# Attention and FFN in one kernel: FFN buffers lent to exponential tiles, one activation table, down weights loaded late, planner constants set again

## The chip, the cores and the metric

The kernel runs on one core of one Trainium2 chip. The metric is the device time of one execution in microseconds (us). "Span" is the time between the first and the last instruction of the profiled execution; it is about 2.1 us shorter than the time of the same run.

Names: PE is the TensorE matmul row, DVE is VectorE, ACT is ScalarE, POOL is GpSimd, SP is the engine that issues most DMAs. PEclk is the granted TensorE clock as a share of full speed.

## The reference, cut to what matters

```python
# x: [1, 2048, 512], bf16.  32 heads of 16.  F = 1376
g = sigmoid((x * gate_w).sum(-1, keepdims=True))
q, k, v = split_heads(x @ wqkv)
a = softmax(q @ k.T * Dh ** -0.5) @ v @ wo          # 32 heads, 2048 x 2048 scores each
b = ((x @ w_gate) * (x @ w_up)) @ w_down
return g * a + (1 - g) * b
```

The exponentials rule: 32 x 2048 x 2048 of them. The kernel works on score tiles of 128 keys by 512 queries; a "quarter" `m` is four heads and 512 queries, and there are 32 quarters of 64 tiles, 2048 tiles in all.

## The kernel before

The kernel is a Python program that plans itself. While it is built, a small list scheduler walks a clock for each engine, decides what each engine does next, and emits the instructions in that order. That fixes the order of each engine, and between engines the program waits on semaphores (in the trace of before ScalarE waits four times, 10.1 us in all, for PV matmuls in the first 200 us).

Of the tiles of each quarter a fourth is meant for VectorE and the rest for ScalarE:

- ScalarE takes two or three score tiles per instruction from PSUM, computes Exp and writes bf16 tiles into "cells" of `PT`. In the plan it has `NA = 3 * 16 * 32 = 1536` tiles.
- VectorE makes the other 512 by integer arithmetic on the bf16 bits: one base tile and three shifted copies, on VectorE and GpSimd. Two such tiles share pairs of cells.
- If VectorE falls behind, a tile of its share is handed over to ScalarE (`convert`).
- The PV matmuls read the cells and free them. ScalarE cannot start while no run of free cells is there (`alloc`).

```python
NMAIN = 54                      # cells in PT, 512 columns each
NCELL = NMAIN + 4               # and the four tiles of wv, once V is done
RA = 26                         # cells 0..25 ScalarE's, 26..53 VectorE's pairs
...
segs = [(0, RA), (NMAIN, 4)]
def alloc(n, t, pair=False, keep=0):
    if pair: ...                # first free pair of cells from RA on
    ...                         # ScalarE: smallest free run of n cells in segs
...
def act_step():                 # ScalarE's step of the planner
    ...
    c = alloc(n, t)
    if c is None:
        return False            # no free cells: ScalarE waits
    old = claim(c, n, 1)        # waits for the PV matmuls that read these cells last
    k = _Task("act", [sc] + old, lambda a: a.activation(cell_ap(c, n), src, ACT.Exp, scale=LN2 / 128.0), ...)
...
lag = lag_()                    # how far VectorE's share is behind ScalarE's
if dleft and lag > LC:
    convert()                   # hand one of VectorE's tiles to ScalarE
```

Projections, the gate, FFN and output projection are "fills": they are put between the score matmuls at positions counted in ScalarE tiles (`ua`), from `F0` (first FFN fill) to `F1`. `FA0` and `FA1` say how late a fill may be before it takes the third score bank of a slot. The gate is one fill of 64 matmuls with one output column each:

```python
for t in range(16):
    for kt in range(4):
        e.matmul(bk.ap[:, t : t + 1], xT[:, kt, t * 128 : (t + 1) * 128], gw[:, kt : kt + 1], ...)
```

The last quarter does without the round trip through memory that spreads the reciprocals in the others (in e1 one took 11.05 us from its first transfer to the multiply). It takes them from a PSUM sum with Ln and Exp, in four blocks:

```python
for tt in range(4):             # four output-projection fills on PE first
    o_first.append(pe_run(deps, fn, ...))
for tt in range(4):
    a1 = now("act", [lastpv, free], lambda a: a.activation(lnd[:, cs], DB.ap[:, cs], ACT.Ln), 0.2)
    a2 = now("act", [a1], lambda a: a.activation(rlast[:, cs], lnd[:, cs], ACT.Exp, scale=-1.0), 0.2)
    mt = now("dve", [a2], lambda v: v.tensor_tensor(OX[..., cs], psO[:, cs], rlast[:, cs], ALU.mult), 0.2)
    o = pe_run([mt], col(banks[tt].ap, OX[..., cs], woz[:, 1, :], False, True), ...)
    combine(4 * c + tt, banks[tt].ap, o)      # DVE: g * a + (1 - g) * b, then the output DMA
```

The softmax here doesn't subtract the row's maximum and nothing guards it: scores larger than these inputs give would overflow.

## Time and profile before

770.96 us, median of 4 runs (769.18 to 773.75). The profiled run took 769.67 us; it is not one of the four.

| what | value | view |
|---|---|---|
| span | 767.6 us | page |
| ACT / PE / DVE busy | 727.6 / 707.3 / 658.8 us | page |
| ACT busy, 0 to 200 us | 172.5 of 200 us | stretches |
| ACT busy, 200 to 700 us | 496.1 of 500 us | stretches |
| tiles on ScalarE | 512 x 2 + 177 x 3 = 1555 | groups by form |
| from the first Ln to the end | 767.6 - 752.15 = 15.45 us | timeline |

From 200 to 700 us ScalarE is busy 99% of the time. This stretch can only get shorter if ScalarE gets fewer tiles. The rest is at the two ends.

The waits of ScalarE in the first 200 us, from the waits view of before (engine, line, whom it waited for: total us, times, longest):

```profile
ACT PT L1446 <- PE psO L1035: 10.1, 4, 4.5
ACT PT L1446 <- PE psS L861: 9.6, 7, 5.9
...
ACT wv L1446 <- PE psS L861: 1.1, 2, 0.6
```

`PE psO L1035` is the PV matmul: ScalarE had scores and waited for a free cell, four times, 10.1 us. `PE psS L861` is the score matmul. 5.9 us of that are the start, which leaves 4.8 us.

ScalarE's exponentials, from the groups by form of before (count, busy us, mean ns, idle before):

```profile
L1446 ACT ACTIVATE PT<-psS 128x1024 bf16<-128x1024 f32 x418 | 422.6, 1128 | 14.6 <-PE psS L861 11.4 <-PE psO L1035 2.9
L1446 ACT ACTIVATE PT<-psS 128x1536 bf16<-128x1536 f32 x154 | 237.8, 1544 | 11.3 <-PE psO L1035 9.2 <-PE psS L861 1.6
L1446 ACT ACTIVATE wv<-psS 128x1024 bf16<-128x1024 f32 x94 | 102.3, 1114 | 2.1 <-PE psS L861 2.0
L1446 ACT ACTIVATE wv<-psS 128x1536 bf16<-128x1536 f32 x23 | 35.9, 1559 | 0.0
L1576 ACT ACT_TABLE_LOAD x4 | 5.1, 1283 | 0.1
L1577 ACT ACT_TABLE_LOAD x4 | 5.1, 1283 | 0.1
```

The tail of before, from its timeline (start, duration, what):

```profile
752.15 0.28 ACT L1576 ACTIVATE oraw<-psS 128x128 f32<-128x128 f32 x1 [1.20 <-PE psS L1046]
...
752.44 1.28 ACT L1577 ACT_TABLE_LOAD   x1
...
753.74 0.31 ACT L1577 ACTIVATE rb<-oraw 128x128 f32<-128x128 f32 x1
...
754.07 1.28 ACT L1576 ACT_TABLE_LOAD   x1
...
755.36 0.28 ACT L1576 ACTIVATE oraw<-psS 128x128 f32<-128x128 f32 x1
...
755.82 0.75 DVE L765 SCALAR_TENSOR_TENSOR ost<-psX,gval,wq 128x512 bf16<-128x512 f32 x1 [1.45 <-PE psX L492]
...
764.72 0.75 DVE L765 SCALAR_TENSOR_TENSOR ost<-psS,gval,wq 128x512 bf16<-128x512 f32 x1 [0.72 <-PE psS L492]
```

Every Ln and every Exp has a table load before it. From the end of Exp (754.05 us) to the start of the next Ln (755.36) are 1.31 us with the load of 1.28 inside. From one Ln to the next are 3.21 us. The first combine (755.82) waits for PE, not for ScalarE.

### The profile page before, as it was taken

The page shows a single profiled execution, that of the slowest core. Times are in us where ns is not written, and L with a number is a line of the kernel's source. Part 1 is how long each engine was busy: PE and PEld are TensorE (multiplying, and loading weights), DVE is VectorE, ACT ScalarE, POOL GpSimd, SP SyncE. Part 2 cuts the span into 40 slices and gives each one's busy share as a digit, 9 for nine tenths or more (in the row PEclk, how much of TensorE's full clock was granted, in tenths as well). Part 3 has the DMA queues.
Part 4 walks back from the last instruction along what each step waited for, and adds up shares of the span by engine and source line. Part 5 has one row for each costly group of instructions (what it writes and reads, how often), then busy time and mean ns, then how long its engine had stood idle before and what let it go on. Part 6 is the DMA issues. An engine that isn't in the chain of part 4 may idle for free. (4 is left out here: it accounts for less than half of the span.)

```text
span 767.6 us, 21608 instructions
## 1 busy us (share of the span) xinstructions
PE 707.3 (92%) x9149; PEld 207.6 (27%) x9149; DVE 658.8 (86%) x1255; ACT 727.6 (95%) x710; POOL 314.4 (41%) x334
## 2 busy tenths in 40 slices
PE   7998988988999999999999999999999998899894
PEld 3323322322222222222222222222222222222221
DVE  3889896689898999999989989898788989989882
ACT  3999988898999999999999999999999999999987
POOL 2534553144434434443434434434433334444430
PEclk9999997999999999999999999999999999999887
DMA  9800000000000010000000100000000100000000
GB/s 185 264 17 2 20 17 19 2 16 20 16 16 13 9 34 30 20 17 17 18 10 13 37 26 17 16 15 20 6 16 21 44 17 19 3 19 15 20 16 28
DMA packets 31015, 21.66 MB, mean 28 GB/s; under 512 B 18344, under 2 KB 25928, under 8 KB 30920
## 3 DMA queue, kind: packets, MB, share of 16 engines
q1 hardware_dynamic: 26936, 18.44, 8.2%
q10 hardware_dynamic: 3984, 1.84, 1.1%
q8 instruction: 73, 1.20, 0.6%
q14 instruction: 22, 0.18, 0.1%
HBM read 15.11 MB, written 2.35 MB: 23 GB/s over the span
## 5 line engine op out<-in xcount | busy, mean ns | idle before, releaser
L1446 ACT ACTIVATE PT<-psS 128x1024 bf16<-128x1024 f32 (+1 forms) x572 | 614.2, 1240 | 25.9 <-PE psS L861 13.0
L978 POOL TENSOR_SCALAR PT<-PT 128x1024 int16<-128x1024 int16 x243 | 256.1, 1055 | 359.7 <-DVE PT L975 226.4
L861 PE MATMUL psS<-QM,KE 32*128 32x512 bf16 x1732 | 272.7, 390 | 15.6 <-ACT PT L1446 7.8
L919 DVE TENSOR_SCALAR PT<-psX 128x512 int16<-128x512 f32 x316 | 216.0, 683 | 46.4 <-PE psS L861 41.6
L1035 PE MATMUL psO<-PT,VS 128*18 128x512 bf16 x1791 | 239.0, 387 | 2.6 <-POOL PT L978 1.0
L1035 PE MATMUL psO<-PT,VD 128*18 128x512 bf16 x1479 | 227.1, 387 | 4.8 <-POOL PT L978 3.4
L975 DVE TENSOR_SCALAR PT<-PT 128x1024 int16<-128x1024 int16 (+1 forms) x498 | 217.2, 476 | 6.6 <-PE psO L1035 1.2
L1446 ACT ACTIVATE wv<-psS 128x1024 bf16<-128x1024 f32 (+1 forms) x117 | 138.2, 1201 | 2.1 <-PE psS L861 2.0
L861 PE MATMUL psX<-QM,KE 32*128 32x512 bf16 x316 | 122.0, 386 | 16.7 <-ACT PT L1446 5.5
L919 DVE TENSOR_SCALAR PT<-psS 128x512 int16<-128x512 f32 x177 | 119.3, 682 | 11.8 <-PE psS L861 8.9
L861 PEld LDWEIGHTS psS<-QM,KE 32*128 32x128 bf16 x1732 | 68.0, 91 | 165.8 <-ACT PT L1446 72.0
L1035 PE MATMUL psO<-wv,VS 128*18 128x512 bf16 x257 | 71.6, 391 | 0.4 <-DVE PT L919 0.2
L1035 PEld LDWEIGHTS psO<-PT,VS 128*18 128x18 bf16 x1791 | 56.4, 89 | 57.5 <-issue 33.9
L861 PEld LDWEIGHTS psX<-QM,KE 32*128 32x128 bf16 x316 | 28.7, 91 | 144.9 <-issue 50.9
L1035 PEld LDWEIGHTS psO<-PT,VD 128*18 128x18 bf16 x1479 | 52.4, 88 | 52.5 <-issue 29.4
L492 PE MATMUL psS<-xT,wu 128*32 128x512 bf16 x672 | 54.5, 389 | 0.5 <-DVE PT L919 0.2
L492 PE MATMUL psS<-wd,hT 128*32 128x512 bf16 (+1 forms) x704 | 52.6, 384 | 1.1 <-DVE PT L919 1.1
L492 PE MATMUL psS<-xT,wg 128*32 128x512 bf16 x672 | 52.8, 385 | 0.8 <-DVE KE L521 0.3
L1107 POOL TENSOR_TENSOR OT<-oraw,rb 128x512 bf16<-128x512 f32 x16 | 20.7, 1293 | 28.7 <-DMA rb<-rscr 23.6
L707 DVE TENSOR_TENSOR hT<-psS,usb 128x512 bf16<-128x512 f32 (+1 forms) x43 | 29.2, 680 | 2.4 <-PE psS L492 2.4
L675 DVE CAST usb<-psS 128x512 bf16<-128x512 f32 (+1 forms) x43 | 29.2, 678 | 1.6 <-PE psS L492 1.5
L1107 POOL TENSOR_TENSOR OX<-oraw,rb 128x512 bf16<-128x512 f32 x15 | 19.5, 1300 | 20.0 <-DMA rb<-rscr 16.3
(87 smaller groups left out, 339.7 us busy)
## 6 DMA issues: line engine op xcount, KB each, us to landing
rb<-rscr SPq DMA_DIRECT2D x31, 256.0 KB
out_dram<-ost SPq DMA_DIRECT2D x16, 128.0 KB, 1.7
wu<-in_B_w_up_dram SPq DMA_DIRECT2D x1, 1376.0 KB, 6.8
wg<-in_B_w_gate_dram SPq DMA_DIRECT2D x1, 1376.0 KB, 10.2
wd<-in_B_w_down_dram SPq DMA_DIRECT2D x1, 1280.0 KB, 12.6
OT<-OX SPq DMA_DIRECT2D x60, 16.0 KB, 1.8
wv<-in_A_wqkv_dram ACTq DMA_DIRECT2D x2, 256.0 KB, 7.6
wo<-in_A_wo_dram SPq DMA_DIRECT2D x1, 512.0 KB, 8.9
```

Source lines behind the costliest of these rows:

```text
L492: return e.matmul(out_ap[32 * q : 32 * q + w, :], lhs[:, 32 * q : 32 * q + w], rhs, start=s0, stop=s1, tile_position=(0, 32 * q), skip_gro ...
L675: lambda v: v.tensor_copy(usb[0:w, n % 2, :], bk.ap[0:w, :]),
L707: lambda v: v.tensor_tensor(hT[0:w, f, :], bk.ap[0:w, :], usb[0:w, n % 2, :], ALU.mult),
L861: r = e.matmul(bk.ap, KE[32 * j : 32 * j + 32, b, kt * 128 : (kt + 1) * 128], QM[32 * j : 32 * j + 32, p, b, :], start=True, stop=True, ti ...
L919: lambda v: v.tensor_scalar(cell_ap(pr["cell"] + i, 1, mybir.dt.int16), bk.ap, CB, 0.0, ALU.add, ALU.max),
L975: fn = lambda v: v.tensor_single_scalar(cell_ap(c, n, I16), cell_ap(pr["cell"], n, I16), 32.0 * k, ALU.add)
L978: fn = lambda g: g.tensor_scalar(cell_ap(c, n, I16), cell_ap(pr["cell"], n, I16), 32.0 * k, 1.0, ALU.add, ALU.mult)
L1035: r = e.matmul(psO[32 * j : 32 * j + VW, :], pv_stationary(m, kt, j, k), cell_ap(cell, 1), start=s0, stop=s1, tile_position=(0, 32 * j), s ...
L1107: lambda e: e.tensor_tensor(dst, oraw[:, s, :], rb[:, s, :], ALU.mult),
L1446: lambda a: a.activation(cell_ap(c, n), src, ACT.Exp, scale=LN2 / 128.0),
```

## The change

The intent:

- `hT` (11 tiles, free until the FFN's first product) and `wd` (11 tiles, free if its load is put off) serve as cells in the first part: `hT` until ScalarE tile 190, `wd` until tile 330.
- One activation table that holds both Ln and Exp is loaded once (in the trace of the changed kernel one load of 1.28 us stands before all of them).
- The down weights are loaded when the plan reaches tile 330 and the lent tiles are free.
- The constants are tuned again. The main cells are split 24 to 30 instead of 26 to 28.

```diff
+    NMAIN = 54
+    C_V = NMAIN
+    C_H = C_V + 4
+    C_D = C_H + FT
+    NCELL = C_D + FT
-    NMAIN = 54
-    NCELL = NMAIN + 4
-    RA = 26
+    RA = 24
...
-        load("sp", wd[:, 0 : FT - 1, :], W_down[0 : (FT - 1) * 128, :]...., "dwd", 0.6, 15.0)
-        d_wd = load("sp", wd[0 : FW[-1], FT - 1, :], W_down[(FT - 1) * 128 : F, :], "dwd", 0.6, 16.0)
...
-        now("act", [o_w0], lambda a: a.activation(warm[:], warm[:], ACT.Exp), 1.6)
+        now("act", [], <load of the table with Ln and Exp>, 1.3)
+        now("act", [o_w0], lambda a: a.activation(warm[:], warm[:], ACT.Exp), 0.3)
...
-        segs = [(0, RA), (NMAIN, 4)]
+        EH = 190
+        ED = 330
+        segs = [(0, RA, 9999), (C_V, 4, 9999), (C_H, FT, EH), (C_D, 5, ED)]
+        prs = [(RA, NMAIN, 9999), (C_D + 5, C_D + FT, ED)]      # pairs for VectorE
...                                                              # alloc skips a segment once ua >= its limit, lent ones come first
+                if c == 0 and f == 0 and not (st["ua"] >= EH and seg_clear(C_H, clock["pe"])):
+                    return [None]                               # first FFN product waits for hT
...
-        F0 = 205.0
-        WP = 32.0
-        F1 = 1490.0
+        F0 = 190.0
+        WP = 40.0
+        F1 = 1500.0
...
-        FA0 = 12
-        FA1 = -99
+        FA0 = 20
+        FA1 = 0
...
+        o_wd = add("sp", [], lambda e: e.dma_start(wd[:, 0 : FT - 1, :], ...), 0.6, lat=12.0, stream="dwd", dma=True, alloc=wd_old)
```

More of the change, by code (lines that the diff above doesn't have):

```diff
@@ L338, in _build @@
         d_wg = load("sp", wg[:, :, :], W_gate.rearrange("(kt p) f -> p kt f", p=128), "dwg", 0.6, 12.0)
-        load("sp", wd[:, 0 : FT - 1, :], W_down[0 : (FT - 1) * 128, :].rearrange("(f p) n -> p f n", p=128), "dwd", 0.6, 15.0)
-        d_wd = load("sp", wd[0 : FW[-1], FT - 1, :], W_down[(FT - 1) * 128 : F, :], "dwd", 0.6, 16.0)
         d_wo = load("sp", wo[:, :, :], A_wo.rearrange("(b p) n -> p b n", p=128), "dwo", 0.6, 18.0)
         o_w0 = now("dve", [], lambda v: v.memset(warm[:], 0.0), 0.07)
-        now("act", [o_w0], lambda a: a.activation(warm[:], warm[:], ACT.Exp), 1.6)
+        now(
+            "act",
+            [],
+            lambda a: a.add_instruction(mybir.InstLoadActFuncSet(name=nc.get_next_instruction_name(), engine=mybir.EngineType.Activation, act_func_set_id=6)),
+            1.3,
+        )
+        now("act", [o_w0], lambda a: a.activation(warm[:], warm[:], ACT.Exp), 0.3)
         o_wrm = now("dve", [], lambda v: v.memset(wrm, 0.0), 0.2)
@@ L387, in _build @@
         cells = [_Cell() for _ in range(NCELL)]
-        for i in range(NMAIN, NCELL):
+        for i in range(C_V, C_H):
             cells[i].need = NB * NCH
+        for i in range(C_H, C_D):
+            cells[i].need = KD
         def cell_ap(c, n, dt=None):
-            if c < NMAIN:
-                a = PT[:, c : c + n, :]
-            else:
-                a = wv[:, c - NMAIN : c - NMAIN + n, :]
+            for buf, lo in ((wd, C_D), (hT, C_H), (wv, C_V), (PT, 0)):
+                if c >= lo:
+                    a = buf[:, c - lo : c - lo + n, :]
+                    break
             a = a.rearrange("p a b -> p (a b)")
@@ L401, in is_free, with pair_starts @@
             return f is not None and f <= t
-        segs = [(0, RA), (NMAIN, 4)]
+        EH = 190
+        ED = 330
+        segs = [(0, RA, 9999), (C_V, 4, 9999), (C_H, FT, EH), (C_D, 5, ED)]
+        prs = [(RA, NMAIN, 9999), (C_D + 5, C_D + FT, ED)]
+        def pair_starts():
+            for lo, hi, lim in prs:
+                if st["ua"] < lim:
+                    for i in range(lo, hi - 1, 2):
+                        yield i
         def alloc(n, t, pair=False, keep=0):
             if pair:
-                got = None
-                for i in range(RA, NMAIN, 2):
+                for i in sorted(pair_starts(), reverse=True):
                     if is_free(i, t) and is_free(i + 1, t):
-                        if got is None:
-                            got = i
                         if keep == 0:
-                            return got
+                            return i
                         keep -= 1
@@ L416, in alloc @@
             best = None
-            for lo, ln in segs:
+            for lo, ln, lim in segs:
+                if st["ua"] >= lim:
+                    continue
                 i = lo
@@ L425, in alloc, with seg_clear @@
                         e += 1
-                    if e - i >= n and (best is None or e - i < best[0]):
-                        best = (e - i, i)
+                    if e - i >= n and (best is None or (lim, e - i) < best[0]):
+                        best = ((lim, e - i), i)
                     i = e
             return None if best is None else best[1]
+        def seg_clear(lo, t):
+            return all(is_free(i, t) for i in range(lo, lo + FT))
         def claim(c, n, need):
@@ L752, in deps @@
                     return [None]
-                return [d_wd, ogate.get("g")] + [ev_h.get((c, f)) for f in range(FT)]
+                return [d_wd[0], ogate.get("g")] + [ev_h.get((c, f)) for f in range(FT)]
             return Fill(f"d{c}.{tt}", packs, deps, evac, pos)
@@ L1172, in _build, with wd_old @@
         fills.sort(key=lambda f: f.pos)
+        d_wd = [None]
+        def wd_old(t):
+            if st["ua"] < ED or not seg_clear(C_D, t):
+                return None
+            old = []
+            for i in range(C_D, C_D + FT):
+                old += cells[i].readers
+            return old
         st = {"ua": 0, "slot": 0, "fill": None, "na": NA, "lastd": None}
@@ L1211, in do_fill @@
                 if f.name[0] == "v":
-                    for i in range(4):
-                        cells[NMAIN + i].readers.append(k)
+                    for i in range(C_V, C_H):
+                        cells[i].readers.append(k)
                 st["fill"] = None
@@ L1224, in ncells @@
             n = 0
-            for c in cells:
+            for i, c in enumerate(cells):
+                if i >= C_H and st["ua"] >= (EH if i < C_D else ED):
+                    break
                 f = c.free_at()
@@ L1411, in filler @@
                 return True
-            fp = sum(1 for i in range(RA, NMAIN, 2) if is_free(i, t) and is_free(i + 1, t))
+            fp = sum(1 for i in pair_starts() if is_free(i, t) and is_free(i + 1, t))
             if nfree < 6 or fp < 2 or not any(AQ):
@@ L1495, in gen_step @@
             return True
+        o_wd = add(
+            "sp",
+            [],
+            lambda e: e.dma_start(wd[:, 0 : FT - 1, :], W_down[0 : (FT - 1) * 128, :].rearrange("(f p) n -> p f n", p=128)),
+            0.6,
+            lat=12.0,
+            stream="dwd",
+            dma=True,
+            alloc=wd_old,
+        )
+        d_wd[0] = add(
+            "sp",
+            [],
+            lambda e: e.dma_start(wd[0 : FW[-1], FT - 1, :], W_down[(FT - 1) * 128 : F, :]),
+            0.6,
+            lat=13.0,
+            stream="dwd",
+            dma=True,
+            alloc=lambda t: None if o_wd.end is None else wd_old(t),
+        )
         for i in range(6):
@@ L1514, in _build @@
             o_last = tp[-1]
+            for i in range(C_H, C_D):
+                cells[i].readers.append(o_last)
             src = psb[kt].ap.bitcast(BF16)[:, 0:512]
```

## The prediction

> **What bounds the kernel now.** ScalarE. Busy (the page): ACT 727.6 of 767.6 us, PE 707.3, DVE 658.8. In the table by stretches ACT is 97 to 100% busy in every 50 us from 200 to 700 us; so the change can win only at the two ends, or by giving ScalarE fewer tiles.

> ScalarE's exponential groups by form hold 512 instructions of two tiles and 177 of three: 1555 tiles. The plan gives it 1536, so 19 of VectorE's 512 tiles were handed over because VectorE's share fell behind. From 15 to 749.7 us, less 22 us idle, a tile costs 0.459 us.

> **Where ScalarE idles.**
> - Ramp, 15 to 200 us: 10.1 us in four waits for PV matmuls (1.4 us at 50 us, 1.1 at 75, 3.1 at 99, 4.5 at 154): waits for a free exponential buffer. Waits for scores after the start are 4.7 us, at 124 to 131 (where PEclk drops to 0.56) and 188 to 193.
> - Tail. The timeline after 752 us shows four rounds of Ln, table load, Exp, table load: loads of 1.283 us, a round 3.2 us. Of eight loads seven are exposed, 9.0 us.

> **The change.**
> 1. Tail. [...] All eight loads vanish. But not 9 us: the first combine (755.8) waits for output-projection matmuls, not ScalarE, and then each quarter is a chain of VectorE multiply 0.29, matmul 0.4 to 0.6, combine 0.75, with gaps about 1.55 to 1.75 us instead of 3.2. The last combine would end near 761.5 instead of 765.5: minus 4 us.
> 2. Ramp buffers. Eleven more tiles until ScalarE tile 190 (about 105 us), eleven more (5 for ScalarE, three pairs for VectorE) until tile 330 (about 170 us). That covers all four buffer waits, 10 us. PE then carries a bigger PV backlog, and hT must be empty before the FFN's first product, so part returns: I count minus 6.
> 3. More pairs for VectorE (15, and 3 for a time, instead of 14): fewer tiles handed over. VectorE made 108 by 200 us where a third of ScalarE's 373 is 124, so most of the 19 fall here. If half stay, ScalarE saves 9 x 0.46 = 4 us.
> 4. Retuned thresholds (fills may be later before they take a score bank): more three-tile exponentials, about 1 us.
> 5. Down weights at about 170 us: 1.28 MB that took 12.6 us to land at the start. They can delay one broadcast of the reciprocals (4.7 us in the chain) and through it GpSimd's queue: plus 1. Taking them out of the start helps nothing that is waited for.

> Sum: 4 + 6 + 4 + 1 - 1 = 14 us on the critical path. Predicted 756.5 us (minus 1.8%), range 748 to 765. Faster by over 2% means below 755.1: chance 0.42; same 0.55; slower 0.03.

> **What would show it.** One table load, not nine; tail rounds of about 1.6 us. ScalarE's waits for PV matmuls before 200 us fall from 10 to under 3 us. ScalarE tiles about 1546, not 1555. Steady stretches unchanged.

> **What would make it wrong.** The buffers only move the wait: ScalarE stalls when hT is taken back near 100 us or wd near 170 us, or PE (95% from 250 us on) becomes the limit and ScalarE waits for scores in 200 to 400 us. Or VectorE's extra tiles make it the limit (95% busy from 250 to 350). Or better: nearly all 19 tiles stay with VectorE and all 10 us are won; then about 749.

## More of the kernel before

From the table by stretches of before (busy us and instruction counts of PE, PEld, DVE, ACT, POOL; then PEclk):

```profile
118.00:120.00 2.00, 1.19 (x22) 0.62 (x20) 0.72 (x2) 2.00 (x3) 1.04 (x1) 1.00 0.06 5
120.00:122.00 2.00, 1.42 (x22) 0.60 (x23) 1.46 (x3) 2.00 (x3) 0.07 (x1) 0.81 0.05 11
...
128.00:130.00 2.00, 2.00 (x18) 0.35 (x19) 1.66 (x3) 1.21 (x2) 1.72 (x2) 0.50 0.10 25
130.00:132.00 2.00, 2.00 (x22) 0.33 (x14) 1.48 (x4) 1.51 (x2) 0.20 (x1) 0.63 0.00 0
```

Between 121 and 131 us the granted TensorE clock is 0.50. Such a stretch is called a dip below. The gate's 64 one-column matmuls run from 116.0 to 125.5 us.

## The result, and the profile after

749.97 us, median of 4 runs (748.14 to 752.36). The ratio to before is 0.9726, with a 95% interval of 0.9686 to 0.9767. Later, with five rounds on another chip (e9 below): 0.9694, 0.9657 to 0.9732.

How ratios are computed: the mean time of one kernel's runs over the mean time of the other's runs of the same rounds, so it is not quite the ratio of the medians that are quoted. Where "us at 771" is said below, it is (1 - ratio) x 771.

The change saved 21 us where 14 were predicted. The time lies inside the range, near its lower end. Of the three classes at 2%, "same" was held likeliest (0.55); the measured class is "faster", to which the prediction gave 0.42.

ScalarE's waits in the first 200 us, from the waits view of the changed kernel (line 1480 is the exponential, 883 the score matmul, 1057 the PV matmul):

```profile
ACT hT L1480 <- PE psS L883: 6.5, 1, 6.5
ACT PT L1480 <- PE psO L1057: 1.6, 1, 1.6
ACT wd L1480 <- PE psS L883: 0.7, 2, 0.5
```

The first line is the start. Waits for cells fell from 10.1 to 1.6 us. Waits for scores after the start fell from 4.8 to 0.7 us; I had not counted on these. They did not all vanish: from 200 to 700 us such waits rose from 1.5 to 6.1 us, and after 700 us they fell from 2.8 to 0.2.

The exponentials of the changed kernel, from its groups by form:

```profile
L1480 ACT ACTIVATE PT<-psS 128x1024 bf16<-128x1024 f32 x374 | 381.3, 1133 | 1.9 <-PE psS L883 1.7
L1480 ACT ACTIVATE PT<-psS 128x1536 bf16<-128x1536 f32 x128 | 201.1, 1571 | 5.2 <-PE psS L883 3.4 <-PE psO L1057 1.6
L1480 ACT ACTIVATE wv<-psS 128x1024 bf16<-128x1024 f32 x121 | 130.2, 1123 | 1.4 <-PE psS L883 1.2
L1480 ACT ACTIVATE hT<-psS 128x1024 bf16<-128x1024 f32 x34 | 36.0, 1149 | 6.6 <-PE psS L883 6.5
L1480 ACT ACTIVATE wd<-psS 128x1024 bf16<-128x1024 f32 x20 | 21.5, 1136 | 0.8 <-PE psS L883 0.7
...
L348 ACT ACT_TABLE_LOAD x1 | 1.3, 1283 | 7.9 <-issue 7.9
```

With the 22 three-tile instructions in `wv`, `wd` and `hT` that are left out here, this is 549 x 2 + 150 x 3 = 1548 tiles, 7 fewer. Three-tile instructions did not rise, as I had thought; they fell from 177 to 150. One table load is left of nine.

The tail of the changed kernel, from its timeline:

```profile
737.10 0.28 ACT L1632 ACTIVATE oraw<-psS 128x128 f32<-128x128 f32 x1 [2.37 <-PE psS L1068]
...
737.41 0.31 ACT L1633 ACTIVATE rb<-oraw 128x128 f32<-128x128 f32 x1
...
740.77 0.75 DVE L787 SCALAR_TENSOR_TENSOR ost<-psX,gval,wq 128x512 bf16<-128x512 f32 x1 [2.73 <-PE psX L512]
...
742.23 0.75 DVE L787 SCALAR_TENSOR_TENSOR ost<-psS,gval,wq 128x512 bf16<-128x512 f32 x1 [0.51 <-PE psS L512]
...
745.36 0.75 DVE L787 SCALAR_TENSOR_TENSOR ost<-psS,gval,wq 128x512 bf16<-128x512 f32 x1 [0.73 <-PE psS L512]
```

The first combine still waits for PE, 3.67 us after the first Ln, as before. Then a round takes 1.46 us (740.77 to 742.23). From the first Ln to the end are 748.3 - 737.10 = 11.2 us instead of 15.45.

Put together on ScalarE, for the two profiled runs:

| part | before | changed | difference |
|---|---|---|---|
| until the first exponential | 14.99 | 16.89 | +1.9 |
| idle between the first and the last exponential | 22.1 | 9.4 | -12.7 |
| tiles x 0.458 us | 1555 | 1548 | -3.2 |
| cost of one tile (0.4582, 0.4577) | | | -0.8 |
| last exponential to first Ln | 2.5 | 2.4 | -0.1 |
| first Ln to the end | 15.45 | 11.2 | -4.3 |
| span | 767.6 | 748.3 | -19.3 |

The idle row is the sum of the idle before the exponentials without the one at the start. The cost of a tile is the time from the first to the last exponential, less the idle, over the tiles. The rows sum to -19.2. The +1.9 at the start is not the change's: when the same kernel was profiled again (e9), its first exponential came at 14.87 us. In the 16.89 us run the last of ScalarE's early DMA issues took 2.16 us, where before it took 0.58.

One pair of profiles is one draw. In e9 the unaltered changed kernel had a span of 740.4 us, 7.9 less than here: the start gave 2.0 of it, and the idle time between the exponentials was 4.4 us where it is 9.4 here. So the table shows where this pair differs; its idle row can move by some 5 us from run to run.

The clock in the same place, from the table by stretches of the changed kernel:

```profile
118.00:120.00 2.00, 1.84 (x21) 0.58 (x21) 2.00 (x6) 2.00 (x3) 0.96 (x1) 0.76 0.09 12
120.00:122.00 2.00, 2.00 (x18) 0.33 (x14) 1.63 (x4) 1.64 (x2) 1.04 (x1) 0.50 0.07 28
122.00:124.00 2.00, 2.00 (x23) 0.57 (x21) 1.37 (x4) 1.67 (x2) 0.33 (x1) 0.89 0.25 98
```

The clock dips to 0.50 for 3.4 us here, 10.2 us before.

### The profile page after: what moved, and what is told of

The parts are those of the page before. It is cut to its first block, busy times and chain, and to the rows that moved or that the text cites. A ratio compares the mean times of both kernels' runs of the same rounds, so it can differ in the third digit from the quotient of the medians.

```text
span 748.3 us, 21637 instructions
## 1 busy us (share of the span) xinstructions
PE 702.9 (94%) x9170; PEld 203.9 (27%) x9170; DVE 660.2 (88%) x1266; ACT 712.9 (95%) x712; POOL 319.3 (43%) x339
## 4 chain that ended last, share of the span: by engine, by line
ACT 53%; PE 29%; DVE 12%; DMA 2%; POOL 1%; issue 1%; ACTq 1%; SPq 0%; POOLq 0%; DVEq 0%
ACT PT L1480 37%; PE psO L1057 9%; ACT wv L1480 9%; PE psS L512 8%; PE psS L883 5%; DVE PT L941 5%; DVE PT L997 5%; ACT hT L1480 4%; PE psX L883 4%; ACT wd L1480 2%; DMA rb<-rscr 1%; ACTq L309 1%; PE psS L1068 1%; PE psX L512 1%; POOL PT L1000 1%
## 5 line engine op out<-in xcount | busy, mean ns | idle before, releaser
L1480 ACT ACTIVATE PT<-psS 128x1024 bf16<-128x1024 f32 (+1 forms) x502 | 543.7, 1244 | 7.1 <-PE psS L883 5.1
L1000 POOL TENSOR_SCALAR PT<-PT 128x1024 int16<-128x1024 int16 x234 | 246.5, 1056 | 308.4 <-DVE PT L997 169.8
L1057 PE MATMUL psO<-PT,VS 128*18 128x512 bf16 x1628 | 226.8, 383 | 0.4 <-POOL PT L1000 0.2
L997 DVE TENSOR_SCALAR PT<-PT 128x1024 int16<-128x1024 int16 x473 | 208.7, 482 | 3.4 <-PE psO L1057 0.9
L1057 PE MATMUL psO<-PT,VD 128*18 128x512 bf16 x1418 | 207.0, 383 | 3.1 <-POOL PT L1000 2.6
L1480 ACT ACTIVATE wv<-psS 128x1024 bf16<-128x1024 f32 (+1 forms) x132 | 147.7, 1162 | 1.4 <-PE psS L883 1.2
L1057 PE MATMUL psO<-wv,VS 128*18 128x512 bf16 x275 | 66.8, 386 | 0.8 <-DVE oraw L1097 0.8
L1057 PEld LDWEIGHTS psO<-PT,VS 128*18 128x18 bf16 x1628 | 51.0, 88 | 46.3 <-issue 31.8
L1057 PEld LDWEIGHTS psO<-PT,VD 128*18 128x18 bf16 x1418 | 47.8, 88 | 46.2 <-issue 27.6
L1480 ACT ACTIVATE hT<-psS 128x1024 bf16<-128x1024 f32 (+1 forms) x39 | 42.2, 1205 | 6.6 <-PE psS L883 6.5
## 6 DMA issues: line engine op xcount, KB each, us to landing
out_dram<-ost SPq DMA_DIRECT2D x16, 128.0 KB, 1.7
```

Source lines behind the costliest of these rows:

```text
L997: fn = lambda v: v.tensor_single_scalar(cell_ap(c, n, I16), cell_ap(pr["cell"], n, I16), 32.0 * k, ALU.add)
L1000: fn = lambda g: g.tensor_scalar(cell_ap(c, n, I16), cell_ap(pr["cell"], n, I16), 32.0 * k, 1.0, ALU.add, ALU.mult)
L1057: r = e.matmul(psO[32 * j : 32 * j + VW, :], pv_stationary(m, kt, j, k), cell_ap(cell, 1), start=s0, stop=s1, tile_position=(0, 32 * j), s ...
```

## The experiments

The theories:

- A: the lent tiles make the gain ahead of the tail, because ScalarE no longer waits for cells.
- B: the retuned constants make it.
- C: the plan is rugged. Small moves of constants give plans several us apart, and the changed kernel is a good draw.

Twelve kernels ran, with five rounds each, in three batches. All were correct. The table has all of them; us at 771 in the last column.

| run | what | median us | ratio to before (95%) | saved |
|---|---|---|---|---|
| changed, first | | 749.97 | 0.9726 (0.9686 to 0.9767) | 21.1 |
| e1 | before + one table | 768.54 | 0.9942 (0.9902 to 0.9981) | 4.5 |
| e2 | e1 + late down weights | 771.82 | 0.9978 (0.9945 to 1.0011) | 1.7 |
| e3 | e2 + new constants | 758.14 | 0.9809 (0.9766 to 0.9853) | 14.7 |
| e4 | e2 + lent tiles | 764.32 | 0.9881 (0.9842 to 0.9920) | 9.2 |
| e5 | e3, constants chosen again | 754.22 | 0.9773 (0.9726 to 0.9819) | 17.5 |
| e6 | changed, FFN start 191 for 190 | 753.26 | 0.9755 (0.9708 to 0.9802) | 18.9 |
| e7 | before, FFN start 206 for 205 | 766.18 | 0.9928 (0.9885 to 0.9971) | 5.6 |
| e8 | changed, other order of the tail | 744.35 | 0.9639 (0.9600 to 0.9679) | 27.8 |
| e9 | changed once more | 748.28 | 0.9694 (0.9657 to 0.9732) | 23.6 |
| e10 | changed, constants chosen again | 740.80 | 0.9607 (0.9577 to 0.9638) | 30.3 |
| e11 | e8 + gate in four parts, constants again | 742.53 | 0.9624 (0.9592 to 0.9656) | 29.0 |
| e12 | e11 + start and output buffers | 739.21 | 0.9588 (0.9554 to 0.9622) | 31.8 |

The medians of before were 774.34 (e1 to e4), 772.95 (e5 to e8) and 770.45 (e9 to e12). Batches ran on different chips, so runs of different batches are compared by their ratios.

### e1: the table alone

```diff
 before
-now("act", [o_w0], lambda a: a.activation(warm[:], warm[:], ACT.Exp), 1.6)
+now("act", [], <load of the table with Ln and Exp>, 1.3)
+now("act", [o_w0], lambda a: a.activation(warm[:], warm[:], ACT.Exp), 0.3)
```

> The kernel before with nothing but the one activation table for Exp and Ln. Theory (chain of the tail): the last rounds shrink from 3.2 to about 1.5 us, so the time falls by 4 us, to about 766.7 (before is 770.9), and nothing ahead of the first Ln moves. Rival (each of the seven exposed loads is worth its full 1.28 us): minus 9 us, 762. Second rival (other table, other speed of Exp): the mean of the two-tile exponentials changes from 1128 ns.

Ratio 0.9942: 4.5 us saved. The profile agrees. The first Ln of e1, from its timeline:

```profile
759.18 0.28 ACT L1582 ACTIVATE oraw<-psS 128x128 f32<-128x128 f32 x1 [2.50 <-PE psS L1052]
```

From there to the end (770.4) are 11.2 us, as in the changed kernel, against 15.45 before. The rival that counted each exposed load in full (9 us) falls. The mean of the two-tile exponentials in `PT` is 1110 ns against 1128, so no cost of the other table shows there.

### e2: the table and the late down weights

```diff
 changed kernel
-EH = 190
-ED = 330                          # and in the test for the load: ua < ED
+EH = 0                            # hT and wd never lent
+ED = 0                            # the load still waits for ua >= 330
-RA, F0, WP, F1, FA0, FA1 = 24, 190, 40, 1500, 20, 0
+RA, F0, WP, F1, FA0, FA1 = 26, 205, 32, 1490, 12, -99
```

> The table and the late load of the down weights, but no FFN buffer ever serves as an exponential tile and every old constant is back. The plan of the other engines is that of before (19 tiles handed over, 512 exponentials of two tiles and 177 of three). My prediction: the late load costs 1 us, so 767 to 768. Rival (taking 1.28 MB out of the start frees the DMA engines for what the first projections need): 2 us or more faster than the run with the table alone, and the first exponential starts earlier than at 15 us. If the load is harmless both ways: equal to the run with the table alone within 0.3%.

Ratio 0.9978, 2.8 us worse than e1, with intervals that overlap. The expected 767 to 768 us (the late load costs 1 us) was missed. Nothing starts earlier: the first exponential is at 15.15 us (e1 15.34), so the rival that hoped for the start falls. The traces show where a cost can come from. The late load was issued in the middle of one quarter's reciprocal round trip, and a step of that round trip took longer than in e1. From the SP timeline of e2:

```profile
175.05 0.54 SPq L1104 DMA_DIRECT2D den<-oraw  x1
175.63 0.48 SPq L1536 DMA_DIRECT2D wd<-in_B_w_down_dram  x1
176.16 0.68 SPq L1546 DMA_DIRECT2D wd<-in_B_w_down_dram  x1
178.41 0.33 SPq L1114 DMA_DIRECT2D rscr<-rec  x1
182.69 0.55 SPq L1122 DMA_DIRECT2D rb<-rscr  x1
```

From `rscr` to `rb` are 4.28 us; in e1 the same pair is 2.75 us apart (180.28, 183.03). From `den` to the multiply that uses the result are 12.8 us (175.05 to 187.85) against 11.05 (176.92 to 187.97). Behind that multiply in GpSimd's fixed order stands a piece of exponential work that TensorE needs: TensorE waited 3.2 us for it until 190.18 us (e1: 1.6 us until 190.47). The next wait of ScalarE for scores ends at 191.38 us after 3.05 us, in e1 at 191.23 after 1.05 us. This is one place and one profiled run each; the cost of about 2 us fits the difference of the times, whose intervals do not settle it. In the changed kernel the load goes out at 176.91 us, after the `rb` of 171.96 us, on which GpSimd's multiply at 176.73 us waited, and lands in 6.2 us. Nobody waits for it there.

### e3 and e4: lent tiles or constants

```diff
 e3: changed kernel                        e4: changed kernel
-EH = 190, ED = 330                       -RA, F0, WP, F1, FA0, FA1 = 24, 190, 40, 1500, 20, 0
+EH = 0, ED = 0 (load at 330 kept)        +RA, F0, WP, F1, FA0, FA1 = 26, 205, 32, 1490, 12, -99
```

> The changed kernel without the borrowed tiles: hT and wd never hold exponentials, all else (table, late wd, new constants, 24 and 30 main tiles) as changed. Theory A (the borrowed tiles make the gain ahead of the tail): the waits of ScalarE for PV matmuls return (about 10 us before 200 us) and the time is 762 to 767. Theory B (the retuned constants make it): 750 to 754. The plan hands over 14 tiles here, 12 in the changed kernel, 19 before; at 0.46 us a tile this alone would put it only 1 us above the changed kernel.

> The changed kernel with the borrowed tiles but every retuned constant set back (26 and 28 main tiles, FFN start 205, end 1490, thresholds 12 and -99, output projections at 32). Theory A (borrowed tiles): ScalarE's waits for buffers stay under 3 us before 200 us and the time is 750 to 756. Theory B (constants): 762 to 767. The plan hands over 24 tiles here, 12 more than the changed kernel, which at 0.46 us a tile costs 5.5 us by itself; so A with this added says 755 to 758.

e3 comes out at 758.14 us (14.7 saved) and e4 at 764.32 us (9.2 saved). For e3 neither theory's number holds (A: 762 to 767, B: 750 to 754). e4 lies in B's range (762 to 767), far from A's; by its ratio it is 761.8 at 771, just under. Against e2, which has neither, the constants alone give 14.7 - 1.7 = 13.0 us and the lent tiles alone 9.2 - 1.7 = 7.5 us. Both together and with e2's 1.7 us would be 22.2; the changed kernel has 21.1 and 23.6. So the two parts add up in these plans, and in this batch each differs from e2 by more than the intervals.

ScalarE's waits for cells in the first 200 us show the lent tiles' share. From the waits views, e2 first:

```profile
ACT PT L1482 <- PE psO L1059: 10.1, 4, 4.5
```

e3, where the constants alone halve it:

```profile
ACT PT L1482 <- PE psO L1059: 4.3, 4, 2.3
ACT wv L1482 <- PE psO L1059: 0.8, 1, 0.8
```

e4, where two waits are left, of which 3.4 us end at 173 us, about when the `wd` tiles are taken back:

```profile
ACT PT L1480 <- PE psO L1057: 3.5, 2, 3.4
```

In e4 the lent tiles save 6.6 us of cell waits; its plan hands over 24 tiles instead of 19, which costs 5 x 0.46 = 2.3 us. That is 4.3 of its 7.5 us. In e3 the constants save 5.0 us of cell waits and 5 handed-over tiles (2.3 us). That leaves 13.0 - 5.0 - 2.3 = 5.7 us. But both profiles caught the slowest of their six runs: the profiled e3 (763.18) is 7.8 us under the profiled e2 (770.94), and the profiled e4 (768.89) only 2.1. So these counts explain the profiled pair of e3 well and that of e4 badly, and the 5.7 us are largely the distance between the profiled run and the mean. Waits for scores after the start fell too: 6.8 us in e2, 4.7 in e3, 4.1 in e4.

### e5, e6, e7: how rugged is the plan?

```diff
 e5: e3                                    e6: changed      e7: before
-F0, WP, F1, FA0 = 190, 40, 1500, 20      -F0 = 190.0      -F0 = 205.0
+F0, WP, F1, FA0 = 212, 44, 1505, 24      +F0 = 191.0      +F0 = 206.0
```

By my account e5's constants are the best of many random draws around the changed kernel's by the planner's own count. No time here is taken from the planner.

> As e3 (no borrowed tiles at all), but with constants chosen again for this layout, as those of the changed kernel were for its own: FFN start 212, end 1505, output projections at 44, threshold 24 instead of 20. Its plan hands over 8 tiles (changed kernel 12, e3 14). Theory A (borrowed tiles carry about 7 us that nothing else gives): at best 756 to 760, and waits for buffers before 200 us stay at 4 us or more. Theory C (the plan is rugged, and the gain ahead of the tail is mostly which plan the constants pick): 748 to 753, level with the changed kernel.

> The changed kernel with one constant moved by one: the FFN starts at tile 191, not 190. The mechanisms (table, borrowed tiles, pairs) are untouched; the plan hands over 16 tiles, not 12, which is 1.8 us by itself. Theory A: 750 to 753. Theory C (rugged plan): 754 or more, with ScalarE waits at other places than in the changed kernel.

> The kernel before with the FFN start at 206, not 205, nothing else. The plan hands over 22 tiles, not 19 (1.4 us). Theory A: within 2 us of before. Theory C: several us away from before, either way; I expect 3 us slower, as before was tuned.

One constant moved by one made the kernel before 5.6 us faster (e7; 2.2 to 8.9 by its interval), although three tiles more were handed over; I had expected 3 us slower. Its waits for cells in the first 200 us are 5.9 us instead of 10.1, with no tile lent: a redraw alone can take away cell waits. The same step took 2.2 to 4.7 us from the changed kernel (0.9755 against 0.9726 and 0.9694), which the intervals do not settle. So C is right in this much: a redraw of the plan can be worth several us, and before was not at its best. With new constants and no lent tile (e5) the kernel saves 17.5 us, 3.6 to 6.1 us less than the changed one. That looked like C for the lent tiles too. e10 was made to check it.

### e9 and e10: lent tiles at equal tuning

```diff
 e10: changed kernel (e9 is the changed kernel unaltered)
-RA, F0, WP, F1, FA0 = 24, 190, 40, 1500, 20
+RA, F0, WP, F1, FA0 = 22, 185, 44, 1490, 28
```

> The changed kernel once more, with five rounds, so that the next three stand beside it on one chip: ratio to before 0.972 to 0.975.

> The changed kernel with its constants chosen again with as many draws as e5 had, so with and without borrowed tiles stand at equal tuning: 22 and 32 main tiles, FFN start 185, end 1490, output projections at 44, threshold 28. Its plan hands over 2 tiles (e5: 8, changed: 12). Theory A (borrowed tiles are worth 7 us that constants cannot give): ratio 0.968 or lower. Theory C (most of the gain ahead of the tail is the draw of the plan): 0.970 to 0.976, within 4 us of e5 (0.977).

e10 saves 30.3 us, 12.8 more than e5, which has no lent tiles and was chosen in the same way. Theory C's forecast (0.970 to 0.976) fails. There are now three pairs with and without them: 7.5 us (old constants, e4 against e2), 6.4 to 8.9 us (the changed constants, e3 against the changed kernel's two ratios), 12.8 us (each with its own best draw). The sign holds in all three. Each side of a pair is one plan, though, and the first two differences are hardly larger than the one redraw of e7; only the third is clearly larger. e10 also drew the split of the main cells anew (22 to 32), which e5 left at 24 to 30. So that lent tiles help is supported by three pairs; how much they help is not settled.

Part of e10's lead over e9 is counted easily: 2 tiles handed over instead of 12, 10 x 0.46 = 4.6 of 6.7 us. e9 itself came out at 0.9694, a little better than the 0.972 to 0.975 expected.

### e8: the order of the tail

```diff
 changed kernel
-PE: wo(0) wo(1) wo(2) wo(3) ox(0) ox(1) ox(2) ox(3);  DVE: mul(0) combine(0) mul(1) combine(1) ...
+PE: wo(0) wo(1) ox(0) wo(2) ox(1) wo(3) ox(2) ox(3);  DVE: mul(0..3) combine(0) combine(1) ...
```

> The changed kernel with the last stage in another order: all four Ln and Exp pairs and the four multiplies first, the output-projection matmuls of quarters 2 and 3 put between the last small matmuls. Everything up to the last PV is the same. If the tail is bound as I read it (first combine waits for all 64 projection matmuls, then rounds of multiply, matmul, combine of 1.46 us), the combines start 1.7 us earlier and follow each other at 0.75 to 1.3 us: 3 to 3.5 us less than the changed kernel. If the tail is bound by ScalarE or the output DMAs: no change.

From the first Ln (734.23) to the end (742.7) are 8.5 us instead of 11.2: 2.7 us, not 3 to 3.5. The end of e8, from its timeline:

```profile
736.61 0.74 DVE L787 SCALAR_TENSOR_TENSOR ost<-psX,gval,wq 128x512 bf16<-128x512 f32 x1
...
737.27 0.74 DVE L787 SCALAR_TENSOR_TENSOR ost<-psS,gval,wq 128x512 bf16<-128x512 f32 x1
...
739.18 1.41 DVE L787 SCALAR_TENSOR_TENSOR ost<-psS,gval,wq 128x512 bf16<-128x512 f32 x2 [1.17 <-DMA out_dram<-ost]
```

The first two combines follow each other at once. The third waits 1.17 us for the output DMA of the first, as there are two output buffers: a new wait behind the old one. By the ratios e8 is 4.2 to 6.7 us under the changed kernel; the 2.7 us of the tail are what the traces show of it, and the rest lies between batches.

### e11 and e12: the gate and the ends

```diff
 e11: e8                                              e12: e11
-one gate fill of 64 matmuls                         -xT copies of block 0: two on DVE, two on ACT
+four gate fills of 16, 24 tiles apart               +all four on DVE
                                                     -ost: two output buffers
                                                     +the last two row blocks use usb (idle by then)
```

The constants were chosen again for each, the limit for lending `hT` included (e12: gate at 210, parts 28 tiles apart, 22 and 32 main cells, FFN start 197, `hT` lent until 200), so both are also new draws of the plan.

> e8 with the gate's 64 one-column matmuls cut into four fills of 16, 24 tiles apart, and constants chosen again for that. If those matmuls, packed in 12 us, are what drops the granted TensorE clock to 0.5 for 3 to 10 us near 120 us, the dip goes, ScalarE's waits for scores there go with it, the mean clock rises to 0.99 in nearly every run, the runs spread less, and the time is 2 to 3 us under e8: ratio about 0.961. If the dip has another cause it stays and the ratio is e8's, 0.964, give or take the draw of the plan.

> e11 with all four copies of the first transposed block on VectorE (in the changed kernel two wait for ScalarE, which is issuing loads until 6.7 us or later; TensorE waits 2.8 to 4.1 us for it) and with two more output buffers for the last two row blocks (in e8 a combine waited 1.2 us for an output DMA). The first exponential comes 2 us earlier, at 13 us, and the end 1 us: ratio about 0.957. If the first scores wait for the loads rather than for ScalarE, the first exponential stays at 15 us.

The clock dip is gone in e11 and e12: every stretch of 1 us from 100 to 159 us is at 1.00. The mean granted clock of their runs is 0.988 to 0.999. e11's ratio is 0.9624, e8's 0.9639, which the intervals do not part, so no gain of the split as such is shown in the time. In e12 the first projections do start earlier (TensorE's first K at 7.47 us, 9.40 in e8), but the first exponential comes at 14.68 us, where 13 was expected. From the timeline of e12:

```profile
12.51 0.69 DVE L611 CAST VS<-psX 128x512 bf16<-128x512 f32 x1
13.29 1.06 POOL L628 TENSOR_SCALAR VD<-VS 128x144 bf16<-128x144 bf16 x3 [9.14 <-DVE VS L611]
13.92 0.40 PE L513 MATMUL psS<-xT,wk 128*32 128x512 bf16 x4 [1.46 <-DMA xT<-in_A_x_dram]
14.25 0.39 PE L895 MATMUL psS<-QM,KE 32*128 32x512 bf16 x2
```

In PE's fixed order a K projection of the next block stands ahead of the first scores, and it waits 1.46 us for its transposed input (0.32 us in e8). So 1.1 of the 1.9 us won turned into this wait. From the first Ln to the end e12 takes 736.2 - 728.50 = 7.7 us, 0.8 less than e8. e12 is the fastest kernel, 31.8 us under before; e10's constants with e12's tail were not run.

### The granted clock and the spread of the runs

The runs of one kernel differ by more than one would like (767.11 to 777.00 for before over three batches). The results list the mean granted TensorE clock of every run. Over the eleven runs of before in each batch it lies between 0.965 and 0.981, and the time falls with it: correlations -0.88, -0.87 and -0.83, slopes of 4.9, 6.9 and 4.3 us per 0.01. This is an association, and it is not everywhere: in the first four runs of the changed kernel the correlation is -0.10. Nor does it say what is cause. A wait elsewhere can come first: in before TensorE waits 1.9 us for GpSimd, until 188.09 us, and the clock drops to 0.50 at 189.5 us. That the dip near 120 us differs between the profiled runs of one plan is the reason to look there.

In the stretches of 1 us from 100 to 159 us of the fourteen traces the clock reads 1.00 or 0.50, apart from those in which a dip starts or ends. The sum of (1 - PEclk) / 0.5 over these stretches is the length of the dip:

| profiled run | gate's matmuls, from to us | dip | waits for scores in the first 200 us, without the start |
|---|---|---|---|
| changed, first | 114.7 to 128.0 | 3.4 us | 0.7 us |
| e9 (the same kernel) | 112.7 to 126.5 | 6.8 us | 1.6 us |
| e8 (same plan up to the tail) | 113.0 to 128.0 | 10.2 us | 2.5 us |
| before | 116.0 to 125.5 | 10.2 us | 4.8 us |
| e2 | 116.4 to 126.1 | 13.6 us | 6.8 us |
| e6 | 113.2 to 129.1 | 17.1 us | 4.4 us |
| e10 | 109.5 to 115.7 | none | 0.3 us, and 1.7 us for the gate itself |
| e11, e12 | in four parts over 46 and 47 us | none | none; 1.3 us |

One stretch of 4 us each from e9, e10 and e11, in this order, from their tables by stretches (the clock is the third figure from the end):

```profile
116.00:120.00 4.00, 4.00 (x35) 0.93 (x35) 3.52 (x9) 3.59 (x4) 1.97 (x2) 0.50 0.09 22
112.00:116.00 4.00, 3.70 (x82) 2.01 (x78) 3.70 (x8) 2.29 (x4) 2.30 (x3) 1.00 0.02 4
116.00:120.00 4.00, 3.89 (x57) 1.25 (x61) 4.00 (x9) 4.00 (x5) 2.09 (x2) 1.00 0.19 67
```

All these dips are one to five times 3.4 us long (3.42, 6.82, 10.24, 13.64 and 17.06). The starts in the trace of before keep such a step too: 121.22, 189.50 and 721.98 us are 68.28 and 532.48 us apart, that is 20 and 156 steps of 3.41 us (an estimate of the step, from these starts and the lengths). In the five runs that the table leaves out (e1, e3, e4, e5, e7) the gate is spread over 9.7 to 14.3 us and the dip is 10.2 to 13.7 us. The first three rows are one plan: each window more at half clock goes with 0.9 us more of ScalarE waiting for scores there, but the time of the whole run does not follow it (spans of 748.3, 740.4 and, with the shorter tail, 742.7 us). The dips near 120 us come with the gate's one-column matmuls when they are strewn over 9.5 us or more. In e10 the same 64 stand within 6.2 us and no dip follows.

The gate is not the only place of dips. In before the clock also stands at 0.50 for 3.4 us from 189.5 us and for 13.6 us from 722 us, where no matmul of the gate runs; with the second go 2.8 us of waits for scores after 700 us. The mean clock counts all of these. What sets them off?

To see, the fourteen traces were cut, from 17 to 735 us, into windows of this 3.41 us at the phase that each trace's own dips mark. TensorE's busy share in each window at full clock was set against the clock of the next.

So in these traces a low busy share of TensorE goes ahead of the dips away from the gate, and a share of 60 to 83% ahead of those at the strewn gate. Why dips followed the four windows at 79 to 83%, where away from the gate none followed 75% and more, is not shown; no run was made for it.

The clock may be one part of what I missed. The mean clock over the runs is 0.9727 in e2, 0.9793 in e3, 0.9848 in e5, 0.9835 in e9 and 0.9912 in e10. At the slope of before in e2's batch (4.9 us per 0.01), an estimate, the step from e2 to e3 is worth 3.2 us, and the step from e9 to e10 3.8 us. This takes the association for a cause, and it overlaps with the waits and tiles counted earlier, so it must not be added to them.

## Why the prediction was right or wrong

The time was in the range and the direction was right. The sum was short by 7 us. The prediction also named a case of about 749 us, in which nearly all 19 tiles stay with VectorE and all 10 us of cell waits are won. The result is close to that number, but by luck: 7 tiles and 8.5 us were won, and the rest came from score waits that no term had.

- "Tail ... minus 4 us": right. 4.25 us in the two profiles, 4.5 us by e1. The chain was right too: the first combine waited for PE, and a round took 1.46 us where "about 1.55 to 1.75" was said. Subtracting table loads (9 us) would have been wrong by half.
- "Ramp buffers ... 10 us. ... part returns: I count minus 6": this term was mis-sized. 8.5 of the 10.1 us of cell waits went and little returned. Taking `hT` back near 100 us cost no wait for a cell at all; at 160 us one of 1.6 us is left. Measured as a part, the lent tiles are worth 7.5 us with the old constants, 6.4 to 8.9 us with the new ones and 12.8 us at equal tuning, one plan on each side.
- "More pairs for VectorE ... 4 us": right in size. Seven tiles fewer are handed over, 7 x 0.458 = 3.2 us. That the pairs are the cause is not shown: e4 has the three lent pairs with the old constants and hands over 24 tiles, five more than before.
- "Retuned thresholds ... more three-tile exponentials, about 1 us": this step failed. Three-tile instructions fell from 177 to 150, and the constants, taken together, are worth 13.0 us (e3 against e2) or 11.9 to 14.4 us (the changed kernel against e4). I read the constants as a knob with one mechanism. They pick a plan, and the plan decides the cell waits, the handed-over tiles and where TensorE idles. My sum had no term for the 4.1 us of score waits that vanished in the first 200 us; they are not the constants' alone, as e3 and e4 both have fewer of them than e2 (4.7 and 4.1 us against 6.8).
- "Down weights ... plus 1": the mechanism is there in e2, where the load falls into a round trip (about 2 us at one wait; times 2.8 us apart with overlapping intervals). In the changed kernel the load falls beside it and costs nothing that the trace shows. "Taking them out of the start helps nothing": right, the first exponential did not come earlier.
- "Steady stretches unchanged": nearly right. ACT is busy 493.6 of 500 us from 200 to 700 us, 496.1 before.

What stays open: which constant does what was not taken apart (e3 changes six). A step of one in one constant moved the time by 5.6 us in e7 (and perhaps 2 to 5 in e6), so single-constant runs would need several draws each. Why lent tiles are worth more at equal tuning (12.8 us) than with the old constants (7.5 us) is not settled: six fewer handed-over tiles in e10 than in e5 are 2.8 us of it, the mean clock differs by 0.0064 besides. That the gate's spread over time causes the dip near 120 us is supported, not isolated: no dip in three plans with another spacing, and a dip in all the others, but e10, e11 and e12 differ from them in other constants too.

## What to carry to other kernels

Cost a removed instruction by the chain that takes its place, not by its duration: eight table loads of 1.28 us were worth 4.5 us. When a change to a self-planned kernel brings new constants, treat "the same change with the old constants" and "the new constants without the change" as two experiments of their own, and move a constant by one in the old kernel to learn what a mere redraw is worth. When the granted clock dips, look at TensorE's busy share in the 3.4 us before: here it was at most 72% away from the gate, and one-column matmuls strewn over 9.5 us or more and a wait of 1.9 us for GpSimd went before dips. And profile the same kernel twice before you explain a few us of one profile: two of the changed kernel differed by 7.9.
